# Strassen products of eight expert rounds put in another order, one round's weight sums and the round count moved forward

## The chip, the cores and the metric

The kernel runs on one core of one Trainium2 chip. The metric is device time in microseconds (us) of one execution, median of several runs. The engines are named as the profile names them: PE (TensorE, matrix products), DVE (VectorE), ACT (ScalarE), POOL (GpSimd) and SP (SyncE, which only starts transfers here). Products go to PSUM, in banks of 512 fp32 columns over 128 partitions; DVE and ACT read and write them there.

## What is computed

A linear attention over 8 batches of 576 tokens, normalised, gives 4608 tokens of width 512. Each token whose skip score is positive goes to one of eight experts of two layers (512 to 1024 to 512), and the result, times a gate, is added to the token.

```python
kv = np.einsum('bhsd,bhse->bhde', k, v)
out = np.einsum('bhsd,bhde->bhse', q, kv)
x = (out / rms * g_norm)                     # then (B,H,S,D) -> (4608, 512)
do_compute = x @ w_skip > 0
xc = x[do_compute]
e_idx = np.argmax(xc @ w_gate, axis=1)       # probs: softmax of the same logits
for e in range(E):
    mask = e_idx == e
    h = np.maximum(xc[mask] @ w1[e], 0.0)
    y[mask] = gate_w[mask, None] * (h @ w2[e])
out[do_compute] = xc + y
```

## The kernel before

The first 143 us or so are the attention, the choice of an expert for each token, and the slot tables; the change leaves them alone. After that come eight rounds, one for each expert, the fullest expert first. Round r holds up to `CAPS[r]` tokens: 352, 352, 320, 288, 288, 288, 256, 256. A loop behind the rounds (`tc.For_i`) takes tokens beyond these caps in further passes; its count `n_rounds` is worked out on the device. With these inputs it makes no pass.

Round 0 uses plain products (`layer_1`, `layer_2`). Rounds 1 to 7 use Strassen's scheme with seven products in place of eight, in both layers.

**Layer 1 of such a round (`fast_1`)** goes over f = 0 to 3, four blocks of 128 hidden columns of one half, and each f owns two PSUM banks, X and Y. The token halves `lo` and `hi` (n columns each, n = half the round's tokens, so 176, 160, 144 or 128) lie side by side in a bank. Each f has seven products of two matmuls each, which this text calls by letters:

| name | product, as the code has it | goes to | then |
|---|---|---|---|
| A | `w(0,0,f)` with `x(0,lo)` | X lo | ACT copies X lo to `p1` |
| B | `ws(1,f)` with `xs(1)` | Y lo | DVE adds `p1` to Y lo; ACT copies Y lo to `u` |
| C | `ws(0,f)` with `xs(0)` | X hi | ACT copies X hi to `p5` |
| D | `ws(2,f)` with `x(1,hi)` | X hi, on top | DVE adds `u` to X hi |
| E | `w(0,1,f)` with `x(0,hi)` | Y lo, on top | DVE writes Y lo + `p5` to Y hi |
| F | `w(1,0,f)` with `x(1,lo)` | X lo, on top | ACT: Relu of all of X to `ht` |
| G | `w(1,1,f)` with `xs(2)` | Y lo, on top | ACT: Relu of all of Y to `ht` |

D adds onto what C left, so it must wait until `p5` is copied. The layer that records the order also makes a product that writes a bank wait for the last ACT or DVE instruction on that bank, even where these touched the other half of it: C waits for the copy of `p1`, F for D's add, G for E's add.

The order of work is the order of the source (`tc.manual_schedule()`), engine by engine, each engine in order. The loop in `fast_1` runs f = 0 to 4 and holds two blocks at once: A, B, C, D of block f and E, F, G of block f - 1. So PE runs, in a middle step: A(f), B(f), E(f-1), C(f), F(f-1), D(f), G(f-1). In the last step, f = 4, `between()` puts the transposes of the next round's tokens (`expert_in`, L889) ahead of G(3).

DVE has other work in the same steps: `do(work, 1)` twice per f takes from `w2_sums` (L935, the weight sums of layer 2, eight jobs), and from f = 2 on come `h_sums` (L929, four instructions that combine finished blocks of `ht`: blocks 0 and 1 after f = 2, block 2 after f = 3, block 3 after f = 4).

**Layer 2 (`fast_2`)** has the same seven products once, each of four matmuls of 256 columns, in the order A, B, C, E, D, F, G. In it DVE takes `beside`: four jobs of `x_sums` (L935) and eight of `w1_sums` (L929, each 128x512), the sums of the next round's tokens and first-layer weights. Then come, in rounds 1 to 5, the tokens beyond 256 with plain products (`layer_2`, L919). `result` (L1107) adds gate times product to the tokens on DVE, and POOL scatters them to `out` (L1110).

What the next round needs of `w1_sums`: B reads its second part, C the first, D, E and G the last ones. `held` (L997) is the ACT copy and `add` (L991) the DVE add of all of this.

Behind round 7 nine small DVE instructions work out the count (`over` to `rnd_i`, L1217 to L1232), and `values_load` (L1235) brings it into a register of each engine; the loop's branch reads it.

Of the kernel before, what the change touches and what calls it, by code (L numbers as in the profile page):

```python
# [17 lines left out]
def kernel(  # L18
# [44 lines left out]
    nc = tc.nc  # L63
# [719 lines left out]
    with tc.tile_pool(name="wpool_b", bufs=1, reuse_waits="tile") as wpool_b, \  # L783
# [216 lines left out]
        def fast_1(r, xt, ht, n, work, between):  # L1000
# [18 lines left out]
            xy = {}  # L1019
            for f in range(HF + 1):  # L1020
                now, was = f < HF, f > 0
                if now:
                    X, Y = bank(), bank()
                    product(X[:, lo], HD, w(0, 0, f), x(0, lo), True)
                    p1 = held(X[:, lo], "p1")
                    product(Y[:, lo], HD, ws(1, f), xs(1), True)
                    add(Y[:, lo], Y[:, lo], p1)
                    u = held(Y[:, lo], "u")
                if was:
                    X_, Y_, p5_ = xy.pop(f - 1)  # L1030
                    product(Y_[:, lo], HD, w(0, 1, f - 1), x(0, hi), False)
                    add(Y_[:, hi], Y_[:, lo], p5_)
                do(work, 1)
                if now:
                    product(X[:, hi], HD, ws(0, f), xs(0), False)
                    p5 = held(X[:, hi], "p5")
                    xy[f] = X, Y, p5
                if was:
                    product(X_[:, lo], HD, w(1, 0, f - 1), x(1, lo), False)
                    nc.scalar.activation(out=ht[:, f - 1, 0:2 * n], in_=X_[:, 0:2 * n], func=ACT.Relu)  # L1040
# [6 lines left out]
                if was:  # L1047
                    product(Y_[:, lo], HD, w(1, 1, f - 1), xs(2), False)
                    nc.scalar.activation(out=ht[:, HF + f - 1, 0:2 * n], in_=Y_[:, 0:2 * n],
                                         func=ACT.Relu)  # L1050
                if f == 2:
                    do(h_sums(r, ht, slice(0, 2)))
                elif f > 2:
                    do(h_sums(r, ht, slice(f - 1, f)))
            do(work)

        def fast_2(r, ht, rest, work, put):
# [73 lines left out]
        def experts(pieces, srcs, xt, ht, yps0, tables, group):  # L1131

            for r in range(E):
# [15 lines left out]
                if r == 0:  # L1149
                    if yps0 is not None:  # L1150
                        tables = first_tables(lambda fs: layer_1(r, xt, ht, slice(P, end), fs), tables)
                        result((0, P, 0), yps0, xgs[0], tables, group)
                    else:
                        layer_1(r, xt, ht, slice(0, end), range(FC))
                    enter(more)
                else:
                    fast_1(r, xt, ht, end // 2, w2_sums(r), lambda: enter(more[0:1]))
                    enter(more[1:])
                if more:
                    n = (more[-1][0] + more[-1][1]) // 2  # L1160
                    beside = x_sums(r + 1, new["xt"], n) + w1_sums(r + 1)
# [5 lines left out]
                else:  # L1167
                    of = {piece[0:2]: piece for piece in todo}
# [3 lines left out]
                if more:  # L1172
                    xt, ht = new["xt"], new_ht()

# [25 lines left out]
        def first_tables(layer, tables):  # L1200
# [3 lines left out]
            for i, t in enumerate((0, half)):  # L1204
# [9 lines left out]

        over = slot_pool.tile([P, E, E], FP32)
        cnt = count_tokens("cnt", slot_pool)
        nc.vector.tensor_tensor(out=over[:, :, :], in0=is_at[:, :, :],  # L1217
                                in1=cnt[:, :].unsqueeze(1).to_broadcast([P, E, E]), op=ALU.mult)
        at_place = slot_pool.tile([P, E], FP32)
        nc.vector.tensor_reduce(out=at_place[:, :], in_=over[:, :, :], axis=AX.X, op=ALU.add)  # L1220
        nc.vector.tensor_tensor(out=at_place[:, :], in0=at_place[:, :], in1=caps[:, :],
                                op=ALU.is_gt)
        rnd = slot_pool.tile([P, 1], FP32)
        nc.vector.tensor_reduce(out=rnd[:, :], in_=at_place[:, :], axis=AX.X, op=ALU.max)
        cmx = slot_pool.tile([P, 1], FP32)
        nc.vector.tensor_reduce(out=cmx[:, :], in_=cnt[:, :], axis=AX.X, op=ALU.max)
        more = slot_pool.tile([P, ROUNDS], FP32)
        nc.vector.tensor_scalar(out=more[:, :], in0=full[:, :], scalar1=cmx[:, 0:1],
                                scalar2=rnd[:, 0:1], op0=ALU.is_lt, op1=ALU.mult)
        nc.vector.tensor_reduce(out=rnd[:, :], in_=more[:, :], axis=AX.X, op=ALU.add)  # L1230
        rnd_i = slot_pool.tile([P, 1], I32)
        nc.vector.tensor_single_scalar(out=rnd_i[:, :], in_=rnd[:, :], scalar=1.0, op=ALU.add)  # L1232
        order.__exit__(None, None, None)

        n_rounds = nc.values_load(rnd_i[0:1, 0:1], min_val=1, max_val=ROUNDS + 1)  # L1235
# [51 lines left out]
```

## Time and profile before

| | us |
|---|---|
| median of 3 runs | 442.76 |
| lowest and highest | 441.32, 446.06 |
| the profiled execution, its time | 440.08 |
| its span, first to last instruction | 438.3 |
| PE busy in the span | 368.8 |
| DVE busy | 250.3 |
| ACT busy | 136.8 |
| POOL busy | 120.6 |
| start of round 1's first product | 193.03 |
| start of the last add of results on DVE | 425.52 |

A row of the timeline gives start, length, engine, line, operation, the tile written and those read, the shape, and how many equal instructions it merges; in brackets stands how long the engine had idled before and what ended that. PE is the matmul, PEld the weight load ahead of it. Each fp32 matmul of the program appears as two in the trace, so a product of layer 1 is a row "x4" and one of layer 2 a row "x8"; neighbours of one form are merged. The length of a PE row is modelled and overlaps the next row, so a product's cost is read from one start to the next.

### The profile page before, as it was taken

Reading aid. Unit: us, or ns where it says so; the run is one execution under the profiler, and the core shown is the slowest. Engines: PE = TensorE matmul, PEld = TensorE weight load, DVE = VectorE, ACT = ScalarE, POOL = GpSimd, SP = SyncE. Lnnn points to the kernel's source line nnn. Section 1 sums busy time; section 2 is a strip of 40 time slices with the busy share of each in tenths; the row PEclk is TensorE's granted clock in tenths of the full one; section 3 lists DMA queues with packets and bytes.
Section 4 is the critical chain, followed back from the end, with each engine's and each line's share of the span. In section 5 each row is a group of like instructions: output and inputs, shape, how many; then the busy total and the mean of one; then the engine's idle time right before and its main releaser. Section 6 shows DMA issues by size and latency. Waiting matters only on the chain.

```text
span 438.3 us, 10443 instructions
## 1 busy us (share of the span) xinstructions
PE 368.8 (84%) x4281; PEld 315.4 (72%) x4281; DVE 250.3 (57%) x621; ACT 136.8 (31%) x365; POOL 120.6 (28%) x185
## 2 busy tenths in 40 slices
PE   0689998698754989989999999999999999997870
PEld 0578886586643949659878887888888888887760
DVE  2115577459896651175655656756656657747530
ACT  1146675446542221203302411421421412413200
POOL 3005677336549060032021303203203103201010
PEclk9869999879785799999999999999999999999995
DMA  7899999974449980635326255455455346201000
GB/s 244 304 390 389 400 399 377 289 276 99 99 133 404 298 295 13 216 99 193 113 104 221 67 194 165 141 191 160 137 192 179 115 191 206 87 1 49 0 24 24
DMA packets 32791, 81.95 MB, mean 187 GB/s; under 512 B 3326, under 2 KB 3330, under 8 KB 32736
## 3 DMA queue, kind: packets, MB, share of 16 engines
q1 hardware_dynamic: 26656, 66.59, 43.2%
q0 software_dynamic: 4576, 14.54, 10.2%
q8 instruction: 35, 0.57, 0.6%
q10 hardware_dynamic: 1504, 0.08, 0.2%
q14 instruction: 20, 0.16, 0.1%
HBM read 66.87 MB, written 14.61 MB: 186 GB/s over the span
## 4 chain that ended last, share of the span: by engine, by line
PE 68%; DVE 15%; issue 4%; DMA 4%; ACT 3%; POOL 2%; DVEq 0%; POOLq 0%; ACTq 0%
PE bank L987 38%; PE bank L919 6%; PE o_ps L402 6%; PE bank L908 5%; PE sum_ps L300 4%; PE q_ps L362 3%; DMA q<-in_q_dram 3%; DVE bank L991 2%; DVE xl L431 2%; DVE hs L929 2%; DVE s L929 2%; DMA wraw<-in_moe_w_gate_dram 2%; DVE w L929 1%; PE g_ps L329 1%; DVE t L935 1%
## 5 line engine op out<-in xcount | busy, mean ns | idle before, releaser
L1110 POOL DMA_INDIRECT out_dram<-xg,rows x16 | 17.4, 1085 | 167.4 <-DVE xg L1107 166.7
L987 PE MATMUL bank<-xt,w 128*128 128x144 f32 (+3 forms) x336 | 55.3, 291 | 0.0
L997 ACT COPY p<-bank 128x144 f32<-128x144 f32 (+4 forms) x70 | 21.0, 300 | 106.1 <-PE bank L987 104.8
L987 PEld LDWEIGHTS bank<-xt,w 128*128 128x128 f32 x336 | 47.0, 191 | 1.4 <-issue 1.4
L991 DVE TENSOR_TENSOR bank<-bank,p 128x144 f32<-128x144 f32 (+4 forms) x70 | 23.0, 338 | 33.1 <-PE bank L987 31.6
L402 PEld LDWEIGHTS o_ps<-kvn,qT 64*64 64x64 f32 (+1 forms) x384 | 28.6, 174 | 15.8 <-issue 7.4
L402 PE MATMUL o_ps<-kvn,qT 64*64 64x73 f32 (+1 forms) x384 | 34.2, 273 | 6.6 <-DVE xl L431 6.2
L464 POOL TENSOR_TENSOR xb<-xl,g_b 128x512 f32<-128x512 f32 x32 | 38.0, 1187 | 0.2 <-issue 0.2
L987 PE MATMUL bank<-xs,s 128*128 128x144 f32 (+3 forms) x224 | 37.6, 292 | 0.2 <-ACT p L997 0.2
L300 PE MATMUL sum_ps<-v,k 64*64 64x64 f32 x1152 | 25.7, 245 | 13.1 <-DMA v<-in_v_dram 10.6
L402 PE MATMUL o_ps<-kvs,qT 64*64 64x73 f32 (+1 forms) x384 | 33.3, 273 | 3.0 <-issue 3.0
L919 PE MATMUL bank<-w,ht 128*32 128x128 f32 (+2 forms) x448 | 34.7, 320 | 0.0
L414 DVE TENSOR_REDUCE rs<-sq 128x8 f32<-128x512 f32 x36 | 24.5, 679 | 17.8 <-ACT sq L406 17.3
L300 PEld LDWEIGHTS sum_ps<-v,k 64*64 64x64 f32 x1152 | 22.6, 156 | 16.1 <-issue 15.3
L987 PEld LDWEIGHTS bank<-xs,s 128*128 128x128 f32 x224 | 31.5, 191 | 1.4 <-ACT p L997 0.6
L879 POOL DMA_INDIRECT xg<-out_dram,src x15 | 15.8, 1052 | 54.2 <-PE bank L987 32.1
L431 DVE TENSOR_TENSOR xl<-o_ps,rs 128x584 f32<-128x584 f32 x36 | 27.6, 767 | 4.8 <-PE g_ps L321 0.5
L987 PE MATMUL bank<-w,ht 128*128 128x256 f32 x112 | 27.2, 386 | 3.7 <-DVE bank L991 3.7
L919 PEld LDWEIGHTS bank<-w,ht 128*32 128x32 f32 (+2 forms) x448 | 21.0, 121 | 12.9 <-issue 9.9
L987 PE MATMUL bank<-xt,s 128*128 128x144 f32 (+3 forms) x112 | 21.5, 314 | 9.5 <-ACT p L997 7.1
L402 PEld LDWEIGHTS o_ps<-kvs,qT 64*64 64x64 f32 (+1 forms) x384 | 27.8, 173 | 0.6 <-ACT rs L421 0.4
L991 DVE TENSOR_TENSOR bank<-bank,u 128x144 f32<-128x144 f32 (+4 forms) x35 | 11.9, 341 | 27.4 <-PE bank L987 27.4
(181 smaller groups left out, 725.7 us busy)
## 6 DMA issues: line engine op xcount, KB each, us to landing
w<-in_moe_w_dram SPq DMA_DIRECT2D x16, 2048.0 KB, 9.2
k<-in_k_dram SPq DMA_DIRECT2D x8, 1152.0 KB, 13.5
v<-in_v_dram SPq DMA_DIRECT2D x8, 1152.0 KB, 15.5
q<-in_q_dram SPq DMA_DIRECT2D x8, 1152.0 KB, 15.9
out_dram<-xb SPq DMA_DIRECT2D x8, 512.0 KB, 9.0
out_dram<-xb POOLq DMA_DIRECT2D x8, 512.0 KB, 7.4
out_dram<-x SPq DMA_DIRECT2D x2, 256.0 KB, 8.5
out_dram<-x POOLq DMA_DIRECT2D x2, 256.0 KB, 6.5
```

The costliest lines, as they stand in the source:

```text
L300: nc.tensor.matmul(out=sum_ps[w * 64:(w + 1) * 64, a, u, :], lhsT=kt[r, 2 * u + w, c, :], rhs=vt[r, 2 * u + w, c, :], start=(c == 0), stop ...
L402: nc.tensor.matmul(out=ps[to, r, cols], lhsT=lhsT, rhs=kv[rows, u, a * KD:(a + 1) * KD], start=True, stop=True, skip_group_check=True)
L414: nc.vector.tensor_reduce(out=rs[:, :, :], in_=sq[:, :, :, :].rearrange("p r w (a d) -> p r (w a) d", a=2), axis=AX.X, op=ALU.add)
L431: nc.vector.tensor_tensor(out=xl[:, :, :, :].rearrange("p r w (a k) -> p r (w a) k", a=2), in0=ps[:, :, 0:2 * PK].rearrange("p r (h k) -> ...
L464: nc.gpsimd.tensor_tensor(out=xb[:, :, 4 * u * D:(4 * u + 4) * D].rearrange("p r (w x) -> p r w x", w=2), in0=xl[:, :, :, G:G + 2 * D], in ...
L908: nc.tensor.matmul(out=hps[:, cols], lhsT=w_sb[r][0][:, dc, f * P:(f + 1) * P], rhs=xt[:, dc, cols], start=(dc == 0), stop=(dc == DC - 1))
L919: nc.tensor.matmul(out=yps[q * m:(q + 1) * m, 0:n], lhsT=ht[:, f, off:off + m], rhs=w_sb[r][1][:, f, q * n:(q + 1) * n], start=(f == 0), s ...
L929: yield lambda to=to, x=x, y=y, op=op: nc.vector.tensor_tensor(out=s[to], in0=x, in1=y, op=op)
L987: nc.tensor.matmul(out=out, lhsT=lhsT(i), rhs=rhs(i), start=start and i == 0, stop=i == k - 1, skip_group_check=True)
L991: nc.vector.tensor_tensor(out=to, in0=x, in1=y, op=ALU.add)
L997: nc.scalar.copy(out=t, in_=x)
L1110: ins = nc.gpsimd.indirect_dma_start(out=cut_rows(m)[:, :], out_offset=bass.IndirectOffsetOnAxis(ap=rows[:, col:col + 1], axis=0), in_=x, ...
```

## The change

Four things change; no arithmetic does.

- In `fast_1`, D of a block moves one step back: the loop now runs A, B, C of block f and D, E, F, G of block f - 1, and PE's order in a middle step is A(f), B(f), D(f-1), E(f-1), C(f), F(f-1), G(f-1). In the last step the transposes come behind F(3), ahead of G(3), with D(3) and E(3) ahead of both. The second `do(work, 1)` of a step stands behind G.
- In `fast_2`, F moves ahead of D: A, B, C, E, F, D, G.
- `w1_sums(1)` runs in round 0 directly behind the first `result`, ahead of the transposes and of layer 2; it used to be the second part of `beside`, among layer 2's pieces. Later rounds keep it in `beside`.
- The count is worked out in round 1, ahead of `fast_2`, in a function `rounds()` with the same nine instructions, and `values_load` stands in round 7 ahead of `fast_2`.

```diff
@@ fast_1
             for f in range(HF + 1):
-                now, was = f < HF, f > 0
+                now, g = f < HF, f - 1
                 if now:
                     X, Y = bank(), bank()
...
-                    u = held(Y[:, lo], "u")
-                if was:
-                    X_, Y_, p5_ = xy.pop(f - 1)
-                    product(Y_[:, lo], HD, w(0, 1, f - 1), x(0, hi), False)
-                    add(Y_[:, hi], Y_[:, lo], p5_)
+                    us[f] = held(Y[:, lo], "u")
+                if g >= 0:
+                    X_, Y_ = banks[g]
+                    product(X_[:, hi], HD, ws(2, g), x(1, hi), False)
+                    add(X_[:, hi], X_[:, hi], us.pop(g))
+                    product(Y_[:, lo], HD, w(0, 1, g), x(0, hi), False)
+                    add(Y_[:, hi], Y_[:, lo], p5s.pop(g))
                 do(work, 1)
                 if now:
                     product(X[:, hi], HD, ws(0, f), xs(0), False)
...
-                if now:
-                    product(X[:, hi], HD, ws(2, f), x(1, hi), False)
-                    add(X[:, hi], X[:, hi], u)
-                else:
-                    between()
+                    if not now:
+                        between()
+                    product(Y_[:, lo], HD, w(1, 1, g), xs(2), False)
...
                 do(work, 1)
-                if was:
-                    product(Y_[:, lo], HD, w(1, 1, f - 1), xs(2), False)
@@ fast_2
             do(work, 1)
+            product(X[:, lo], HF, h(1, 0), w(1, lo), False)
+            do(work, 2)
             product(X[:, hi], HF, hs(2), w(1, hi), False)
             add(X[:, hi], X[:, hi], u)
-            do(work, 2)
-            product(X[:, lo], HF, h(1, 0), w(1, lo), False)
             put((0, P), X)
@@ experts
+                    do(w1_sums(r + 1))
                     enter(more)
...
-                    beside = x_sums(r + 1, new["xt"], n) + w1_sums(r + 1)
+                    beside = x_sums(r + 1, new["xt"], n) + (w1_sums(r + 1) if r else [])
...
+                    if yps0 is not None and r == 1:
+                        rnd_i = rounds()
+                    if yps0 is not None and r == E - 1:
+                        n_rounds.append(nc.values_load(rnd_i[0:1, 0:1], min_val=1,
+                                                       max_val=ROUNDS + 1))
                     of = {piece[0:2]: piece for piece in todo}
                     fast_2(r, ht, todo[2:], beside,
```

PE, round 7, the step f = 1 of layer 1; the number of a bank tells X and Y of the two blocks apart. Before, X and Y of block 0 are 4260 and 4261, those of block 1 are 4280 and 4281:

```order
L987 MATMUL bank_4260<-xt_4053,s1_4197 128x128 x2
L987 MATMUL bank_4280<-xt_4053,w1_4046 128x128 x2
L987 MATMUL bank_4281<-xs_4196,s1_4197 128x128 x2
L987 MATMUL bank_4261<-xt_4053,w1_4046 128x128 x2
L987 MATMUL bank_4280<-xs_4196,s1_4197 128x128 x2
L987 MATMUL bank_4260<-xt_4053,w1_4046 128x128 x2
L987 MATMUL bank_4280<-xt_4053,s1_4197 128x128 x2
L987 MATMUL bank_4261<-xs_4196,w1_4046 128x128 x2
```

Now block 0 has 4276 and 4277, block 1 has 4293 and 4294:

```order
L987 MATMUL bank_4293<-xt_4069,w1_4062 128x128 x2
L987 MATMUL bank_4294<-xs_4212,s1_4213 128x128 x2
L987 MATMUL bank_4276<-xt_4069,s1_4213 128x128 x2
L987 MATMUL bank_4277<-xt_4069,w1_4062 128x128 x2
L987 MATMUL bank_4293<-xs_4212,s1_4213 128x128 x2
L987 MATMUL bank_4276<-xt_4069,w1_4062 128x128 x2
L987 MATMUL bank_4277<-xs_4212,w1_4062 128x128 x2
```

Before, D(0) (the first row) stood ahead of A(1), right behind C(0), and D(1) (the seventh row) two places behind C(1). Now D(0) is the third row, behind A(1) and B(1), and F(0) and G(0) close the step.

DVE, round 4, from the sums of blocks 0 and 1 (hs, 128x256) to those of block 2 (hs, 128x128); "bank<-bank,p" is an add of B or E, "bank<-bank,u" one of D. Before:

```order
L929 TENSOR_TENSOR hs<-ht,hs 128x256
L991 TENSOR_TENSOR bank<-bank,p_3893 128x144
L991 TENSOR_TENSOR bank<-bank,p_3873 128x144
L935 TENSOR_TENSOR t_3805<-w_3546,t_3805 128x512
L991 TENSOR_TENSOR bank<-bank,u 128x144
L935 TENSOR_TENSOR t_3805<-w_3546,t_3805 128x512
L929 TENSOR_TENSOR hs<-ht 128x128
L929 TENSOR_TENSOR hs<-hs,ht 128x128
L929 TENSOR_TENSOR ht<-ht 128x128
L929 TENSOR_TENSOR hs<-ht,hs 128x128
L991 TENSOR_TENSOR bank<-bank,p_3906 128x144
```

Now:

```order
L929 TENSOR_TENSOR hs<-ht,hs 128x256
L991 TENSOR_TENSOR bank<-bank,p_3906 128x144
L991 TENSOR_TENSOR bank<-bank,u 128x144
L991 TENSOR_TENSOR bank<-bank,p_3889 128x144
L935 TENSOR_TENSOR t_3821<-w_3562,t_3821 128x512 x2
L929 TENSOR_TENSOR hs<-ht 128x128
L929 TENSOR_TENSOR hs<-hs,ht 128x128
L929 TENSOR_TENSOR ht<-ht 128x128
L929 TENSOR_TENSOR hs<-ht,hs 128x128
L991 TENSOR_TENSOR bank<-bank,u 128x144
L991 TENSOR_TENSOR bank<-bank,p_3922 128x144
```

The add of D(3), ahead of the sums of block 2 before, now stands behind them, directly ahead of E(3)'s.

DVE, from the first results of round 0 to the first add of round 1 (L991); s is the tile of `w1_sums`. Before:

```order
L1107 SCALAR_TENSOR_TENSOR xg_211<-bank,gate,xg_211 128x512 x2
L935 TENSOR_TENSOR xs<-xt 128x2x176
L935 TENSOR_TENSOR xs<-xt,xs 128x2x176
L935 TENSOR_TENSOR xt<-xt 128x2x176
L935 TENSOR_TENSOR xs<-xt,xs 128x2x176
L1107 SCALAR_TENSOR_TENSOR xg_211<-bank,agate,xg_211 128x256
L929 TENSOR_TENSOR s_2694<-w_2530 128x512 x2
L929 TENSOR_TENSOR s_2694<-s_2694,w_2530 128x512 x2
L1107 SCALAR_TENSOR_TENSOR xg_211<-bank,agate,xg_211 128x128
L929 TENSOR_TENSOR w_2530<-w_2530 128x512 x2
L929 TENSOR_TENSOR s_2694<-w_2530,s_2694 128x512 x2
L991 TENSOR_TENSOR bank<-bank,p_2794 128x176
```

Now:

```order
L1106 SCALAR_TENSOR_TENSOR xg_211<-bank,gate,xg_211 128x512
L929 TENSOR_TENSOR s_2674<-w_2530 128x512 x2
L929 TENSOR_TENSOR s_2674<-s_2674,w_2530 128x512 x2
L929 TENSOR_TENSOR w_2530<-w_2530 128x512 x2
L929 TENSOR_TENSOR s_2674<-w_2530,s_2674 128x512 x2
L1106 SCALAR_TENSOR_TENSOR xg_211<-bank,gate,xg_211 128x512
L935 TENSOR_TENSOR xs<-xt 128x2x176
L935 TENSOR_TENSOR xs<-xt,xs 128x2x176
L935 TENSOR_TENSOR xt<-xt 128x2x176
L935 TENSOR_TENSOR xs<-xt,xs 128x2x176
L1106 SCALAR_TENSOR_TENSOR xg_211<-bank,agate,xg_211 128x256
L1106 SCALAR_TENSOR_TENSOR xg_211<-bank,agate,xg_211 128x128
```

The eight jobs of `w1_sums` that stood between the last pieces of round 0 and the first add of round 1 now stand behind the first result.

More of the change, by code (lines that the diff above doesn't have):

```diff
@@ L1035, in fast_1 @@
                     product(X[:, hi], HD, ws(0, f), xs(0), False)
[L1036 to L1045 removed]
+                    p5s[f] = held(X[:, hi], "p5")
+                if g >= 0:
+                    product(X_[:, lo], HD, w(1, 0, g), x(1, lo), False)
+                    nc.scalar.activation(out=ht[:, g, 0:2 * n], in_=X_[:, 0:2 * n], func=ACT.Relu)
+                    if not now:
+                        between()
+                    product(Y_[:, lo], HD, w(1, 1, g), xs(2), False)
+                    nc.scalar.activation(out=ht[:, HF + g, 0:2 * n], in_=Y_[:, 0:2 * n],
+                                         func=ACT.Relu)
                 do(work, 1)
[L1047 to L1050 removed]
                 if f == 2:
@@ L1212 @@
         experts(plan, (src, asrc), xt0, ht0, yps0, (rows, arows), "first")
[L1215 to L1232, printed above, removed]
         order.__exit__(None, None, None)
-        n_rounds = nc.values_load(rnd_i[0:1, 0:1], min_val=1, max_val=ROUNDS + 1)
+        n_rounds = n_rounds[0]
         colid = slot_pool.tile([P, NCOL], I32)
```

25 lines of the change are left out of this document (24 added, 1 removed).

## Prediction

> **What bounds the kernel now.** I read the page first, for the share of each engine and for the chain that ended last.
>
> ```profile
> PE 368.8 (84%) x4281; PEld 315.4 (72%) x4281; DVE 250.3 (57%) x621; ACT 136.8 (31%) x365; POOL 120.6 (28%) x185
> ...
> PE 68%; DVE 15%; issue 4%; DMA 4%; ACT 3%; POOL 2%; DVEq 0%; POOLq 0%; ACTq 0%
> PE bank L987 38%; PE bank L919 6%; PE o_ps L402 6%; PE bank L908 5%; PE sum_ps L300 4%; PE q_ps L362 3%; DMA q<-in_q_dram 3%; DVE bank L991 2%; DVE xl L431 2%; DVE hs L929 2%; DVE s L929 2%; DMA wraw<-in_moe_w_gate_dram 2%; DVE w L929 1%; PE g_ps L329 1%; DVE t L935 1%
> ```
>
> PE carries the chain, and the Strassen products (L987) alone are 38% of it. The DVE pieces in the chain (L991, hs, s, w, t) are the places where PE stood still between those products. The view of waits on PE says what for:
>
> ```profile
> PE bank L987 <- ACT p L997: 7.4, 13, 2.4
> PE bank L987 <- DVE bank L991: 6.6, 14, 0.9
> PE bank L987 <- DVE t L935: 2.3, 1, 2.3
> ```
>
> That is 16.3 us in 28 waits. The true loss is larger: a matmul row is modelled, and the wait and the restart are better seen from start to start. So I read the timeline of PE in one round, round 4, with n = 144.
>
> ```profile
> 333.65 1.34 PE L987 MATMUL bank<-xs,s 128*128 128x144 f32 x8
> 335.52 0.76 PE L987 MATMUL bank<-xt,s 128*128 128x144 f32 x4 [0.52 <-ACT p L997]
> ...
> 341.21 0.65 PE L987 MATMUL bank<-xs,s 128*128 128x144 f32 x4
> 341.70 0.65 PE L987 MATMUL bank<-xt,w 128*128 128x144 f32 x4
> 342.29 0.76 PE L987 MATMUL bank<-xt,s 128*128 128x144 f32 x4
> 342.89 0.65 PE L987 MATMUL bank<-xs,w 128*128 128x144 f32 x4
> ...
> 345.34 0.65 PE L987 MATMUL bank<-xt,w 128*128 128x144 f32 x4
> 346.35 0.76 PE L987 MATMUL bank<-xt,s 128*128 128x144 f32 x4 [0.36 <-ACT p L997]
> 346.94 0.65 PE L987 MATMUL bank<-xs,w 128*128 128x144 f32 x4
> ...
> 348.41 0.60 PE L889 MATMUL bank<-ident,xg 128*128 128x128 f32 x4
> 349.38 0.76 PE L987 MATMUL bank<-xs,w 128*128 128x144 f32 x4 [0.37 <-DVE bank L991]
> 349.97 0.60 PE L889 MATMUL bank<-ident,xg 128*128 128x128 f32 x4
> 350.41 1.89 PE L987 MATMUL bank<-w,ht 128*128 128x256 f32 x8
> ...
> 355.59 1.89 PE L987 MATMUL bank<-t,ht 128*128 128x256 f32 x8
> 357.32 1.89 PE L987 MATMUL bank<-w,hs 128*128 128x256 f32 x8
> 359.73 2.00 PE L987 MATMUL bank<-w,ht 128*128 128x256 f32 x8 [0.52 <-DVE bank L991]
> 361.56 1.89 PE L987 MATMUL bank<-t,ht 128*128 128x256 f32 x8
> ```
>
> An undisturbed product takes one step of 0.49 us (341.21 to 341.70). Every "xt,s" row is a D, behind F in the old order (behind C in the first step). What each place loses, in order:
>
> - D(0) was due two steps after 333.65, at 334.63, and came at 335.52: 0.9 late.
> - D(2) came 0.59 after F(1), and the product behind it 0.60 after D(2): 0.10 of waiting and 0.10 of restart, 0.20. D(1) is the same case.
> - D(3) came 1.01 after F(2): 0.52, with the restart 0.62.
> - G(3) came 0.97 after four transposes, which take 0.44 (349.97 to 350.41): 0.53, with the restart 0.63.
> - In layer 2 a step is 1.73 (355.59 to 357.32). F came 2.41 behind D, and G 1.83 behind F: 0.68 and 0.10, so 0.78.
>
> **The change, part by part. Layer 2.** F waits for D's add because both use bank X. With F ahead of D nothing of that is left: the next product on D's bank is in no hurry, G writes Y, and E's add on Y has D and F ahead of it, two steps. The add of D and the result of X then lie beside G's 1.73 us. Seven rounds at 0.78: **5.5 us gone**. What is late next is the result of Y behind G, as now.
>
> **The start of a round.** D(0) waits for a chain on DVE and ACT (last weight sums, B(0)'s add, copy u, copy p5). Now A(1) and B(1) stand ahead of it, two steps of work. Round 4 had 0.9 to hide and gets 0.98 of cover. Round 7 has more than that:
>
> ```profile
> 395.17 1.29 PE L987 MATMUL bank<-xs,s 128*128 128x128 f32 x8
> 398.81 0.71 PE L987 MATMUL bank<-xt,s 128*128 128x128 f32 x4 [2.35 <-ACT p L997]
> 399.36 0.61 PE L987 MATMUL bank<-xt,w 128*128 128x128 f32 x4
> ...
> 193.73 1.64 PE L987 MATMUL bank<-xs,s 128*128 128x176 f32 x8
> 197.68 0.86 PE L987 MATMUL bank<-xt,s 128*128 128x176 f32 x4 [2.31 <-DVE t L935]
> 198.38 0.76 PE L987 MATMUL bank<-xt,w 128*128 128x176 f32 x4
> ```
>
> In round 7 the step is 0.45 (0.55 from 398.81 to 399.36, less 0.10), D(0) is 2.7 late, and two steps cover 0.9 of it. I take 0.9 for each of rounds 2 to 7: **5.4 us**. The lower end is 0, if the products that now stand in the gap are themselves held up.
>
> Round 1 (the last three rows) has a step of 0.60, so D(0) was due at 194.93 and came at 197.68: 2.75, with the restart 2.85. There the weight sums themselves leave the boundary.
>
> ```profile
> 143.40 1.66 SPq L271 DMA_DIRECT2D w<-in_moe_w_dram  x1
> ...
> 187.65 0.75 DVE L1107 SCALAR_TENSOR_TENSOR xg<-bank,gate,xg 128x512 f32<-128x512 f32 x1 [7.29 <-PE bank L919]
> ...
> 191.67 1.28 DVE L929 TENSOR_TENSOR s<-w 128x512 f32<-128x512 f32 x2
> ```
>
> Eight sums at 0.64 are 5.1 us, and their new place is the 7.29 us in which DVE idled ahead of 187.65. Their weights were asked for at 143.40, 37 us before that idle time begins. So they are hidden, and **2.85 us go**. If the weights were late, DVE would stand in front of the next result and the term would fall towards 0; the distance of 37 us speaks against it.
>
> **Inside layer 1.** D(1), D(2), D(3) have four products between them and their copy now, so 0.20, 0.20 and 0.62 go, and so does G(3)'s 0.63: 1.65 a round. Two new waits come. F now needs D's add, and G needs E's add, each three steps earlier.
>
> ```profile
> 343.16 0.32 DVE L991 TENSOR_TENSOR bank<-bank,u 128x144 f32<-128x144 f32 x1 [0.84 <-PE bank L987]
> ...
> 345.49 0.52 DVE L991 TENSOR_TENSOR bank<-bank,p 128x144 f32<-128x144 f32 x2
> ```
>
> From D(2)'s start at 342.29 to the end of its add at 343.48 are 1.19, of which 0.10 is the restart: 1.09 against three steps of 1.47. With DVE free this costs nothing; DVE is not free behind the block sums. (a) In step 3 the adds of B(3) and D(2) come behind the sums of blocks 0 and 1, which end at 345.49, 2.60 after G(1). Two adds take 0.52, the way to PE 0.06: F(2) can start 3.18 after G(1), and is due six steps, 2.94, after it: 0.24, with the restart 0.34. (b) In step 4 the add of D(3) comes behind the sums of block 2. Today the first product behind those is G(3), 2.44 after G(2) (346.94 to 349.38). Now it is F(3), due three steps, 1.47, after G(2): 0.97, with the restart 1.07, and the transposes that softened it stand behind F(3). So 1.41 a round comes back, 0.24 is left, and over seven rounds **1.7 us go**. The bounds are 11.6 (none of the new waits) and a loss of 3.8 (both twice as long, against 1.65 gone).
>
> Row 349.38 shows the place where a rule bears on this: the product waits for an add that itself waits behind sums it does not need. The Trainium skill, TensorE: Matmul & The Clock Gate, section on the array's architectural detail, says that VectorE's queue is strictly first in, first out. By that rule the 1.07 in step 4 stands, and with it the sum below; if DVE could take D(3)'s add first, seven times 1.07 more would go and the time would be 420.5. The trace agrees with the rule.
>
> **The count.** On each engine a register load is added ahead of layer 2 of round 7, and nine small DVE instructions move into layer 2 of round 1, where DVE waits for the first product anyway; I cost those at nothing.
>
> ```profile
> L1235 PEldq TENSOR_LOAD <-rnd_i x1: 736/736/736, 428.1 to 428.1; - x1
> ...
> 426.54 0.98 POOL L1110 DMA_INDIRECT out_dram<-xg,rows  x1 [0.74 <-DVE cnt L595]
> ...
> DMA to landing us min/median/max: 2.6/3.3/7.7
> ...
> L1238 POOLq EVENT_SEMAPHORE  x16: 17/43/96, 429.0 to 432.3; - x16
> ```
>
> PE's queue stands still for the load, 0.74, with nothing beside it: **0.7 us added** (0 if queued matmuls cover it, 1.5 if the restart doubles it). At the end I expect no gain: POOL reaches its waits for transfers at 429.0, and the last scatter, issued at 426.54, lands at 429.1 at the earliest by the shortest landing, 2.6. Without the count POOL would only wait there longer.
>
> **The sum.** 5.5 + 5.4 + 2.85 + 1.7 - 0.7 = 14.7 us. The profiled execution took 440.08, which gives 425.4. It lies 2.7 below the median of the three runs shown, 442.76, and the change should be seen there: **428.0 us**.
>
> **Rivals.**
>
> - *The starts give back what they gain.* DVE now has two weight sums between B(0)'s add and B(1)'s; if the products behind D(0) then wait for them, 5.4 us stay: 433.4. Against it: D(0)'s add is due about 1.1 after D(0), and two sums of 0.68 fit ahead of it. 0.14.
> - *The three-step window is too short* (slower). F and G wait in each of 28 blocks, 56 times. The spare time is 1.47 - 1.15 = 0.32, for n = 128 about 0.27. It decides where the way from a product to the next one over DVE is longer than three steps: each 0.1 beyond costs 0.2 with the restart, 11 us in all, and 0.34 a time makes the kernel slower than 447. The rows give 1.15 with DVE free, so this needs DVE behind in every block, and it is behind only after the block sums. 0.04.
> - *The clock.* The view of stretches has the granted clock ahead of the last two columns: half in parts of the attention, whole in the rounds:
>
> ```profile
> 83.00:94.00 11.00, 9.71 (x174) 8.42 (x174) 3.60 (x10) 3.72 (x11) 3.66 (x7) 0.53 1.03 381
> ...
> 333.00:350.00 17.00, 15.75 (x124) 14.58 (x118) 12.31 (x32) 6.51 (x20) 3.65 (x4) 1.00 0.55 173
> ```
>
> Ten us at half clock cost about 5 us of PE time; three such stretches in the rounds would eat the gain, 443. 0.03. The Trainium skill, same page, Part 1, says that activity releases the clock and idle windows lower it; by that rule a PE that waits less keeps its clock and this rival is out. No round here tests it.
>
> - *The end is shorter after all*: the nine instructions and the load leave POOL's path, 1.3 us from 427.5 to 428.8: 426.7. The landing speaks against it. 0.08.
> - *The new waits inside layer 1 are milder*, half of 1.41 in each of seven rounds: 423.1. 0.06.
>
> **How the numbers follow.** The main case has 0.65, with a range of its own of 425.5 to 430.5. The range for all, 423.5 to 433.5, reaches to the starts that give nothing on one side and most of the way to the milder waits on the other; the two bounds of the load lie inside. Something over 1% (4.4 us) can be told from no change here. Faster by more than that is every case but the window and the clock, less a little for a sum of small misses: 0.92; within 1%: 0.04; slower: 0.04.
>
> **What would show it.** F 1.73 behind E and D 1.73 behind F in layer 2, with no wait; D(0) of round 1 without a wait, of rounds 2 to 6 too, and of round 7 with some 1.7 left; D(1) to D(3) with none. New waits of F(3), about 1 us a round, for DVE, and smaller ones of F(2) from round 3 on. The last scatter to the end of the span as long as before, 11.8 us. The prediction is wrong if F and G wait in steps 1 and 2, if D(0) still waits in rounds 2 to 6, or if a round runs below the full clock.

## The result, and the profile after

| | before | changed |
|---|---|---|
| median, us | 442.34 of 4 runs | 429.49 of 4 runs |
| lowest, highest | 441.32, 446.06 | 428.29, 432.58 |
| profiled execution, its span | 440.08, 438.3 | 429.86, 428.1 |
| round 1's first product to the end of the span | 245.3 | 230.8 |

The ratio is 0.9705, 95% interval 0.9629 to 0.9782: faster, and 1.5 us above the 428.0 forecast, inside the main case's own range.

The last row of the table is worked out from the first product A(0) of round 1. These are the rows of the timeline of PE, the first of the kernel before, the others of the changed one:

```profile
193.03 0.86 PE L987 MATMUL bank<-xt,w 128*128 128x176 f32 x4
```

```profile
197.31 0.86 PE L987 MATMUL bank<-xt,w 128*128 128x176 f32 x4
...
199.86 0.76 PE L987 MATMUL bank<-xs,s 128*128 128x176 f32 x4
200.46 0.76 PE L987 MATMUL bank<-xt,s 128*128 128x176 f32 x4
```

A(0) started 4.3 us later in the changed kernel's profile. The sums that were moved into round 0 did not do that: from the first product of round 0's second layer to A(0) are 37.37 us in both (155.66 to 193.03 before, 159.94 to 197.31 now), so the delay comes from ahead of it. In the twelve other profiles read below and above A(0) started anywhere from 192.3 to 199.9. The profiled run of e8, below, was a slow one (435.79 us), but what it lost lies ahead of its A(0) at 199.92, and its layer 1 took the 117.1 of the changed kernel. That scatter lies in every median; the time behind A(0) does not have it, and there the change won 245.3 - 230.8 = **14.5 us**, against 14.7 in the forecast's sum. The row at 200.46 is D(0), 0.60 behind B(1) (199.86), as every product there: no wait is left in it.

The view of waits on PE had 28 waits and 16.3 us on these products before, now:

```profile
PE bank L987 <- DVE bank L991: 6.0, 9, 0.8
PE bank L987 <- ACT p L997: 1.5, 1, 1.5
```

The timeline of PE in round 5 shows which. (The rows that the prediction showed for n = 144 and called round 4 are round 5's as well; rounds 3 to 5 have the same sizes.)

```profile
330.56 0.65 PE L987 MATMUL bank<-xs,s 128*128 128x144 f32 x4
331.05 0.65 PE L987 MATMUL bank<-xt,s 128*128 128x144 f32 x4
331.54 0.65 PE L987 MATMUL bank<-xt,w 128*128 128x144 f32 x4
...
338.89 0.65 PE L987 MATMUL bank<-xs,s 128*128 128x144 f32 x4
339.62 0.76 PE L987 MATMUL bank<-xt,w 128*128 128x144 f32 x4
...
341.20 0.65 PE L987 MATMUL bank<-xt,w 128*128 128x144 f32 x4
342.66 0.76 PE L987 MATMUL bank<-xt,w 128*128 128x144 f32 x4 [0.81 <-DVE bank L991]
...
349.80 1.89 PE L987 MATMUL bank<-t,ht 128*128 128x256 f32 x8
351.53 1.89 PE L987 MATMUL bank<-w,ht 128*128 128x256 f32 x8
353.25 1.89 PE L987 MATMUL bank<-w,hs 128*128 128x256 f32 x8
354.98 1.89 PE L987 MATMUL bank<-t,ht 128*128 128x256 f32 x8
```

D(0) at 331.05 comes one step of 0.49 behind B(1) and E(0) one step behind it: the start waits for nothing. F(2) at 339.62 is 0.24 late, F(3) at 342.66 comes 1.46 behind E(3), 0.97 late; with the restart of 0.10 that is 0.34 and 1.07, the two new waits of the forecast to the digit. In layer 2 E, F, D, G follow each other at 1.73.

From starts like these, the length of each layer in each round, in us (layer 2 with the plain products behind it, in round 7 up to the start of its last matmul):

| | r1 | r2 | r3 | r4 | r5 | r6 | r7 | sum |
|---|---|---|---|---|---|---|---|---|
| layer 1 before | 21.76 | 18.49 | 17.57 | 17.45 | 17.35 | 16.58 | 17.71 | 126.90 |
| layer 1 changed | 18.92 | 17.61 | 16.43 | 16.43 | 16.32 | 15.32 | 16.07 | 117.12 |
| layer 2 before | 18.46 | 16.58 | 14.86 | 14.86 | 14.86 | 12.88 | 12.66 | 105.17 |
| layer 2 changed | 17.67 | 15.79 | 14.07 | 14.07 | 14.07 | 12.09 | 11.87 | 99.62 |

Layer 1 won 9.8, layer 2 5.5, together 15.3. Since 14.5 came out, 0.8 were lost behind the last product. The view of transfers, cut to the time from the last scatter's issue to its landing, shows it; before, and below it changed:

```profile
q0 software_dynamic: 145, 0.37, 36.4%
issues: line engine op xcount, KB each, median us to landing
out_dram<-xg,rows POOLq DMA_INDIRECT x1, 2.6
```

```profile
q0 software_dynamic: 160, 0.43, 33.8%
q8 instruction: 1, 0.02, 1.6%
q14 instruction: 1, 0.01, 0.5%
issues: line engine op xcount, KB each, median us to landing
out_dram<-xg,rows POOLq DMA_INDIRECT x1, 3.4
```

The columns behind a queue are packets, MB and share of time. With the count in the registers early, the branches behind the rounds run early and fetch their code (the two rows "instruction") while the scatter is under way; it lands after 3.4 and not 2.6. From the moment POOL sees the landing to the end of the span both have 9.1.

### The profile page after: what moved, and what is told of

Its sections match the earlier page's. It is cut to its first block, busy times and chain, and to the rows that moved or that the text cites. A ratio compares the mean times of both kernels' runs of the same rounds, so it can differ in the third digit from the quotient of the medians.

```text
span 428.1 us, 10435 instructions
## 1 busy us (share of the span) xinstructions
PE 360.0 (84%) x4281; PEld 313.1 (73%) x4281; DVE 249.8 (58%) x621; ACT 137.4 (32%) x365; POOL 120.8 (28%) x185
## 5 line engine op out<-in xcount | busy, mean ns | idle before, releaser
L987 PE MATMUL bank<-xt,w 128*128 128x144 f32 (+3 forms) x336 | 57.7, 294 | 6.2 <-DVE bank L991 6.0
L991 DVE TENSOR_TENSOR bank<-bank,p 128x144 f32<-128x144 f32 (+4 forms) x70 | 23.6, 337 | 36.5 <-PE bank L987 35.7
L879 POOL DMA_INDIRECT xg<-out_dram,src x15 | 16.7, 1113 | 53.5 <-PE bank L987 31.7
L919 PEld LDWEIGHTS bank<-w,ht 128*32 128x32 f32 (+2 forms) x448 | 21.0, 121 | 12.9 <-issue 9.9
L448 POOL TENSOR_TENSOR lp<-xl 128x36 f32<-128x36 f32 x36 | 9.2, 255 | 70.6 <-DVE xl L431 70.3
L365 ACT COPY qT<-q_ps 128x512 f32<-128x512 f32 x32 | 18.8, 587 | 28.4 <-PE q_ps L362 28.2
L406 ACT ACTIVATE sq<-o_ps 128x512 f32<-128x512 f32 x36 | 21.5, 597 | 19.5 <-PE o_ps L402 19.3
```

What stands on the lines that cost most here:

```text
L365: nc.scalar.copy(out=qT[:, :, :, :].rearrange("p w a t -> p (w a t)"), in_=ps[:, :, :, :, :].rearrange("p w a h t -> p (w a h t)"))
L406: nc.scalar.activation(out=sq[:, :, :, :], in_=heads(ps, G, G + 2 * D), func=ACT.Square)
L919: nc.tensor.matmul(out=yps[q * m:(q + 1) * m, 0:n], lhsT=ht[:, f, off:off + m], rhs=w_sb[r][1][:, f, q * n:(q + 1) * n], start=(f == 0), s ...
L987: nc.tensor.matmul(out=out, lhsT=lhsT(i), rhs=rhs(i), start=start and i == 0, stop=i == k - 1, skip_group_check=True)
L991: nc.vector.tensor_tensor(out=to, in0=x, in1=y, op=ALU.add)
```

## The experiments

Eleven runs followed, e11 the changed kernel once more. The table has what was measured, in us; "part" is round 1's first product to the end of the span, "end" the last scatter's issue to the end of the span, both of the profiled run.

| kernel | median | ratio to before, 95% | part | layer 1 | layer 2 | end |
|---|---|---|---|---|---|---|
| changed | 429.49 | 0.963 to 0.978 | 230.8 | 117.1 | 99.6 | 12.6 |
| e1_count_late | 424.83 | 0.954 to 0.970 | 230.0 | 117.1 | 99.6 | 11.8 |
| e2_l2_old | 431.19 | 0.969 to 0.983 | 236.2 | 117.1 | 105.2 | 12.5 |
| e3_l1_old | 435.82 | 0.976 to 0.993 | 240.1 | 126.4 | 99.7 | 12.6 |
| e4_sums_back | 427.20 | 0.960 to 0.973 | 232.3 | 118.7 | 99.6 | 12.5 |
| e5_sums_behind | 422.56 | 0.942 to 0.955 | 227.8 | 110.8 | 103.0 | 12.5 |
| e6_sums_early | 427.16 | 0.953 to 0.967 | 232.8 | 115.5 | 103.3 | 12.5 |
| e7_both | 420.59 | 0.939 to 0.954 | 225.6 | 108.4 | 103.3 | 12.4 |
| e8_load_late | 430.86 | 0.958 to 0.973 | 234.0 | 117.1 | 103.0 | 12.4 |
| e9_best | 416.63 | 0.937 to 0.947 | 220.6 | 107.7 | 99.6 | 11.8 |
| e10_delay | 425.20 (1 run) | - | 230.7 | 117.1 | 99.6 | 12.5 |
| e11_changed_again | 425.75 | 0.958 to 0.969 | 230.3 | 117.1 | 99.6 | 12.1 |

They ran in three groups, e1 to e4, e5 to e8 and e9 to e11, each on one chip with its own runs of the kernel before. e5 to e8 all have 1.1 us more in layer 2 of each of rounds 3 to 5; e8, whose rounds are those of the changed kernel, has it too, so e5 to e7 are set against e8 and its 234.0.

**The parts one by one. e1_count_late** undoes the early count:

```diff
-                    if yps0 is not None and r == 1:
-                        rnd_i = rounds()
-                    if yps0 is not None and r == E - 1:
-                        n_rounds.append(nc.values_load(rnd_i[0:1, 0:1], min_val=1,
-                                                       max_val=ROUNDS + 1))
...
+        rnd_i = rounds()
         order.__exit__(None, None, None)
...
-        n_rounds = n_rounds[0]
+        n_rounds = nc.values_load(rnd_i[0:1, 0:1], min_val=1, max_val=ROUNDS + 1)
```

> The changed kernel with the count alone put back: its nine DVE instructions behind the last result, its register loads behind everything. Three theories of the early count. (a) It brings nothing at the end and costs 0.7 us on PE, as forecast: then the time from round 1's first product to the end of the span becomes 230.1, 0.7 less than the 230.8 of the changed kernel. (b) The load lies under the queued matmuls and costs nothing, but the branches now fetch their code while the last scatter is under way and hold its landing up: then layer 2's first product still starts one step, 0.45, behind the last product of layer 1 in round 7, as it does with the load in between; the last scatter lands 2.6 behind its issue as in the kernel before, not 3.4, and from its issue to the end of the span are 11.8, not 12.6; 230.0. (c) The landing varies by itself and the early count is worth nothing either way: 230.8, with a landing anywhere between 2.6 and 3.6, and kernels that keep the early count show landings of 2.6 too.

Theory (b) in each number: the part is 230.0, the end 11.8, the landing 2.6, and no instruction fetch lies between issue and landing. Layer 1 is as long without the load as with it, so the load cost nothing.

**e2_l2_old** has the old `fast_2`, D ahead of F.

> The changed kernel with layer 2 alone in the old order, F behind D. The theory: F waits for D's add in each of seven rounds, 0.78 a round with the restarts, and nothing else moves: 5.5 us slower than the changed kernel, some 435. The rival is that the starts of the rounds take part of it back, since the sums beside layer 2 get 0.78 more time: then D(0) of round 7 waits less, 1.0 in place of 1.7, and the loss is 4.8. The last scatter keeps the early count: by the collision it lands 3.4 behind its issue again, by chance alone anywhere from 2.6.

Layer 2 is the kernel before's to the hundredth, 105.17, and layer 1 the changed kernel's, round 7 (16.07) among it: 5.4 us in the part, and nothing handed on to the starts. Its last scatter landed after 3.3, again with a code fetch beside it.

**e3_l1_old** has the old `fast_1`.

> The changed kernel with layer 1 alone in the old order, D ahead of the copies of the next step. The theory: the starts of rounds 2 to 7 lose their 5.0 us again, and the inside of layer 1 its 1.9; round 1, whose weight sums have left the boundary, loses little at its start, 0.2 to 0.9 in place of 2.85: 7 to 8 us slower than the changed kernel, some 437. The rival, that the weight sums alone did the whole work of round 1, has the start of round 1 as good as in the changed kernel, and the loss at 6.9; that the order of layer 1 did it has the start 2.8 slower and the loss at 9.7.

9.4 us, more than the theory's 7 to 8. Round 1 lost 0.71 (19.63 to 18.92): neither 0 nor 2.8, so the moved sums and the new order shared that start. The view of the timeline, D(0) of round 1:

```profile
196.20 1.42 PE L987 MATMUL bank<-xs,s 128*128 128x176 f32 x8
198.02 0.86 PE L987 MATMUL bank<-xt,s 128*128 128x176 f32 x4 [0.39 <-ACT p L997]
```

Two steps of 0.60 behind the first row would be 197.39; it is 0.63 late, and 0.10 go to the restart. Rounds 2 to 6 lost 5.4. Round 7 lost 3.2, and half of that has another cause. First two rows of its timeline, then the view of stretches, with the granted clock ahead of the last two columns:

```profile
394.44 0.71 PE L987 MATMUL bank<-xt,s 128*128 128x128 f32 x4 [2.36 <-ACT p L997]
...
396.27 1.06 PE L987 MATMUL bank<-xt,w 128*128 128x128 f32 x4
```

```profile
394.40:398.80 4.40, 4.36 (x24) 4.36 (x25) 2.19 (x6) 0.80 (x3) 0.00 (x0) 0.62 0.00 0
```

Behind D(0)'s wait of 2.36 the clock fell to 0.62 on average, and four products took 0.85 apiece in place of 0.45: 1.6 us. Without that the loss is 7.8, inside the theory's band. Last, the load. Here G(3) had waited, and the load began with it; the load, then the products:

```profile
L1172 PEldq TENSOR_LOAD <-rnd_i x1: 488/488/488, 408.9 to 408.9; - x1
```

```profile
408.91 0.71 PE L987 MATMUL bank<-xs,w 128*128 128x128 f32 x4 [0.85 <-DVE bank L991]
409.62 1.97 PE L987 MATMUL bank<-w,ht 128*128 128x256 f32 x8
```

Layer 2 starts 0.71 behind G(3), where a step and a restart are 0.55: the same load of 0.49 that costs nothing in the changed kernel costs 0.16 here.

**e4_sums_back** puts `w1_sums(1)` back into `beside`.

> The changed kernel with round 1's weight sums back at the boundary. The theory: the two products that now stand ahead of D(0) cover two steps of 0.60 of the 2.75 that it was late, so D(0) of round 1 waits 1.55 and 0.1 for the restart: 1.65 us slower than the changed kernel. The rival: the order of layer 1 alone covers all of it and moving the sums was worth nothing: 0. The other rival: the products that stand in the gap are held up too: 2.85 slower.

Round 1's layer 1 took 20.52 for 18.92, 1.6, and nothing else moved: the theory. So of the 2.84 won in round 1 the order alone is worth 1.24 (21.76 to 20.52), the sums alone 2.13 (21.76 to 19.63), and they overlap by half a us: each hides part of the same wait.

**What delays the last scatter. e8_load_late** computes the count early and loads it behind the rounds.

> The changed kernel with the count computed early but loaded into the registers at the end, as in the kernel before. It tells which half of the early count delays the last scatter. If it is the branches, which run as soon as the registers are loaded: 11.8 from the last scatter's issue to the end of the span and a landing after 2.6, and 230.0 from round 1's first product. If it is the moved DVE instructions: 12.6, with a landing after 3.4, and 230.8.

12.4, as with the early load. The run did not decide: with the count known since round 1 the loads waited for nothing, so they and the branches still ran ahead of the scatter. **e10_delay** makes them wait:

```diff
...
+        wide = slot_pool.tile([P, 512], FP32, name="wide")
+        nc.vector.memset(wide[:, :], 0.0)
+        for _ in range(3):
+            nc.vector.tensor_tensor(out=wide[:, :], in0=wide[:, :], in1=wide[:, :], op=ALU.add)
+        rnd_i = slot_pool.tile([P, 1], I32)
+        nc.vector.tensor_single_scalar(out=rnd_i[:, :], in_=n_rounds[0][:, :], scalar=1.0, op=ALU.add)
...
```

> The changed kernel with eight of the count's nine DVE instructions early, the ninth and the register loads at the end behind some 2 us of idle work on DVE (a fill and three additions on 128x512, which no result uses). If the code that the branches fetch is what delays the last scatter: the fetch comes after the last packet, the packets end 2.3 behind the issue and not 2.8 to 3.0; from the issue to the end of the span 11.8, or more by as much as the idle work outlasts the landing. If the early DVE instructions or the loads in themselves are the cause: 2.8 to 3.0 again.

The view of transfers from issue to landing, the loads' rows under it:

```profile
q0 software_dynamic: 160, 0.43, 42.4%
issues: line engine op xcount, KB each, median us to landing
out_dram<-xg,rows POOLq DMA_INDIRECT x1, 2.6
```

```profile
L1247 PEldq TENSOR_LOAD <-rnd_i x1: 488/488/488, 413.5 to 413.5; - x1
```

Eight of the nine DVE instructions are early, the loads come 2.5 behind the issue (410.99), no fetch lies beside the packets, and they land after 2.6. So the fetched code delays the scatter, not the DVE instructions. Nor do the loads: in the changed kernel the last of them began at 403.5, 12 us ahead of the scatter. The end is 12.5 all the same, since the idle work outlasts the landing. Of the profiles, each with the branches early has an end of 12.1 to 12.6 and a fetch beside the packets; each with the count late (before, e1, e9) has 11.8 and none.

**What the new waits are. e5_sums_behind** puts the block sums behind the adds:

```diff
                     add(Y_[:, hi], Y_[:, lo], p5s.pop(g))
-                do(work, 1)
+                    if g > 0:
+                        do(h_sums(r, ht, slice(g - 1, g)))
+                do(work, 2)
...
-                if f == 2:
-                    do(h_sums(r, ht, slice(0, 2)))
-                elif f > 2:
-                    do(h_sums(r, ht, slice(f - 1, f)))
+            do(h_sums(r, ht, slice(HF - 1, HF)))
```

> The changed kernel with the block sums of h behind the adds: the sums of block f - 1 come in step f + 1 (block 0 in step 2, 1 in step 3, 2 in step 4) behind D's and E's adds and not ahead of them, and the weight sums of w2 are all issued by step 2. The theory: F(2) and F(3) wait only because D(2)'s and D(3)'s adds stand behind those sums in DVE's queue, so both waits go: 7.4 us for F(3) and 2.2 for F(2) over the seven rounds, 9.6 in all; 221.2 from round 1's first product to the end of the span. Rival one: the adds wait for PE and ACT and not for the sums; then nothing changes, 230.8. Rival two: block 2's sums now push block 3's back, and the second product of layer 2, which needs them, waits; at one block's sums, 1.05, a round, 7.4 come back and 228.6 are left.

No wait for the adds is left in the view, and layer 2 waits for no sums: both rivals fall. But 6.2 us were won (against e8), not 9.6. The timeline of PE in round 5, then that of DVE:

```profile
335.68 0.65 PE L987 MATMUL bank<-xt,s 128*128 128x144 f32 x4
336.17 1.40 PE L987 MATMUL bank<-xt,w 128*128 128x144 f32 x8
337.41 0.60 PE L889 MATMUL bank<-ident,xg 128*128 128x128 f32 x4
```

```profile
335.36 0.28 DVE L929 TENSOR_TENSOR hs<-ht,hs 128x128 f32<-128x128 f32 x1
336.44 0.32 DVE L991 TENSOR_TENSOR bank<-bank,u 128x144 f32<-128x144 f32 x1 [0.79 <-PE bank L987]
336.93 0.32 DVE L991 TENSOR_TENSOR bank<-bank,p 128x144 f32<-128x144 f32 x1 [0.17 <-PE bank L987]
337.16 0.28 DVE L929 TENSOR_TENSOR hs<-ht 128x128 f32<-128x128 f32 x1
```

DVE now idles ahead of D(3)'s add at 336.44. E(3) and F(3) are merged in the row at 336.17, and the transposes come 1.24 behind its start where two steps are 0.98: 0.26 of F(3) stays. In the last step no A, B, C stand between; F(3) is only two steps behind D(3), 0.98 against the 1.09 to 1.15 of the way over DVE. Seven times 0.25 are 1.8 of the missing 3.4. Another 1.2 came back in rounds 6 and 7 (0.68 and 0.78 won in place of 1.33, the two waits of 1.61 less the 0.28 that stays): there three sums of w2 now stand ahead of B(1)'s and D(0)'s adds, and F(0) comes 0.3 and 0.4 late with its restart. The transposes of round 6 come 0.3 late too, and the load in round 7 costs 0.15: it began at 395.3, hardly ahead of G(3) at 395.36, and layer 2 starts 0.60 behind G(3) where a step is 0.45. Some 0.3 are a late F(0) in rounds 3 to 5.

**e6_sums_early** issues all sums for the next round inside layer 2, four each behind A, B and E.

> The changed kernel with the sums for the next round (four of x, eight of w1) all issued inside layer 2, four behind each of A, B and E, and none behind the last result. The theory: D(0) of round 7 waits 1.63 and 0.1 for the restart because four sums are left over behind round 6's results, so it goes: 1.7 us faster, 229.1. A second part: the 0.1 of C at the start of rounds 2 to 6 goes with it, 0.5 more. The rival: the larger blocks of sums now stand ahead of E's and D's adds in layer 2 and G or the results wait, 0.1 to 0.6 a round: between nothing and 3 us slower.

Round 7's layer 1 fell from 16.07 to 14.34, the 1.73 of the theory; C's 0.1 stayed. Round 1's layer 2 rose by 0.29, E waiting for the larger block once, and layer 1 of round 4 by 0.15: 1.2 net in the part.

**e7_both** has the two.

> Both of these together, on the changed kernel. If they are independent: 9.6 and 1.7 to 2.2 us, some 219.3 from round 1's first product to the end of the span, PE with no wait of over 0.2 us left in the rounds. The rival is that DVE becomes the bound: PE no longer gives it the time that it lost in waits, 1.4 a round, and waits show up at the starts of the rounds; then 2 to 7 us less are won.

8.4 us against e8: all that the two won alone (7.4) and 1.0 more, but 3 less than the 11.3 to 11.8 expected. The loss is not that of the rival: the view of waits on PE lists none for DVE in the rounds, and D(0) of round 7 comes one step behind B(1). Of the missing 3 us, 1.8 are the 0.25 of F(3) in seven rounds, which e5 had left already. The two are independent, and DVE did not become the bound.

**e9_best** takes e7 and adds the late count, one sum of w2 fewer in step 0, and the first transposes ahead of F(3) (the lines of e5, e6 and the count are left out here):

```diff
-                do(work, 1)
...
+                do(work, 2 if f else 1)
...
                 if g >= 0:
+                    if not now:
+                        between()
                     product(X_[:, lo], HD, w(1, 0, g), x(1, lo), False)
                     nc.scalar.activation(out=ht[:, g, 0:2 * n], in_=X_[:, 0:2 * n], func=ACT.Relu)
-                    if not now:
-                        between()
```

> A version meant to beat both: the sums behind the adds and early in layer 2 as in the kernel before this one, the count at the end, the first four transposes of the next round ahead of F(3) and not behind it, so that D(3)'s add has two products and 0.44 us of transposes to end in, and one sum of w2 fewer in step 0. On the other hand the time from round 1's first product to the end of the span was 225.6 for the two moves alone on a chip on which three pauses of 1.05 in the small products of rounds 3 to 5 are part of it. The theory: 0.25 a round of F(3) goes in six rounds, 1.5; up to 0.4 of F(0) in each of rounds 6 and 7; 0.7 at the end: 222.6 with the pauses, 219.4 without. The rival is that G(3) or the sums of the last block are now late and layer 2's second product waits: 0.2 to 0.5 a round back, some 225.

The median is 416.63, ratio 0.9419 (0.9369 to 0.9470), and the changed kernel on the same chip 425.75: it beats the kernel before and the changed one. The part is 220.6 where 219.4 was expected. The row of busy shares on its page, then all that the view of waits on PE lists in the rounds:

```profile
PE 359.1 (86%) x4281; PEld 313.5 (75%) x4281; DVE 254.0 (61%) x649; ACT 138.1 (33%) x365; POOL 119.4 (29%) x185
```

```profile
PE bank L889 <- DMA xg<-out_dram,src: 0.8, 2, 0.5
```

What is late next is the gather of the next round's tokens, for which the transposes now wait; round 6 took 15.15 where e7 had 14.49, and in rounds 6 and 7 F(2) comes 0.2 late again.

**e11_changed_again** is the changed kernel once more.

> The changed kernel itself, on the chip of the two kernels before. From round 1's first product to the end of the span 230.8 if the chip has no pauses in the small products of rounds 3 to 5, 234.0 if it has them; the packets of the last scatter end 2.8 to 3.0 behind its issue; layer 1 of the seven rounds takes 117.1 in all either way. If the rounds of the changed kernel vary from run to run by more than 0.3, the differences read so far are less sure than they look.

Layer 1 was 117.13 and layer 2 99.62, against 117.12 and 99.62, and no round differs by more than 0.03. Differences of 0.1 between rounds can be trusted. The end was 12.1 and the landing 3.0, so the fetch costs between 0.3 and 0.8 from run to run; its packets ended 2.5 behind the issue, earlier than expected.

## Why the prediction was right

| term of the sum | forecast | measured |
|---|---|---|
| layer 2, seven rounds | 5.5 | 5.5 |
| start of round 1 | 2.85 | 2.8 |
| starts of rounds 2 to 7 | 5.4 | 5.0 |
| inside layer 1 | 1.7 | 1.9 |
| register load on PE | -0.7 | 0 |
| the end | 0 | -0.8 (-0.3 in e11) |
| sum | 14.7 | 14.5 |

The measured terms are rounded; the 14.5 is 245.3 - 230.8.

**Layer 2** held in each number, and e2 shows it stands alone. **Round 1**: the forecast had the sums do it all; e3 and e4 show the sums worth 2.1 alone and the order 1.2. The number held because the order hides the 0.7 that the sums alone would have left; the forecast did not count on that, so here it was lucky. **Rounds 2 to 7**: each start won 0.7 to 0.95. The step "I take 0.9 for each" was too large by C's own restart of 0.10, which the forecast took to go and which stays. Round 7 kept a wait, now 1.63 and the restart, as said:

```profile
388.11 0.61 PE L987 MATMUL bank<-xs,s 128*128 128x128 f32 x4
390.19 0.71 PE L987 MATMUL bank<-xt,s 128*128 128x128 f32 x4 [1.47 <-ACT p L997]
```

**Inside layer 1** the two new waits came where and as long as worked out; in rounds 1 and 2 they were smaller (no F(2) wait in round 1), in 6 and 7 larger. That they hang on the order of DVE's queue was argued from one row; e5 shows it: with the sums behind the adds both go, down to the 0.25 that the two steps leave. That F(3) stands only two steps behind D(3) the forecast did not see; behind the longer wait for the sums it made no difference. The Trainium skill, TensorE: Matmul & The Clock Gate, section on the array's architectural detail, has VectorE's queue as strictly first in, first out; the runs agree.

**The load** was the mis-sized term. "PE's queue stands still for the load, 0.74, with nothing beside it" failed: the rows of the changed kernel, the load first,

```profile
L1171 PEldq TENSOR_LOAD <-rnd_i x1: 485/485/485, 401.4 to 401.4; - x1
```

```profile
401.73 0.61 PE L987 MATMUL bank<-xs,w 128*128 128x128 f32 x4
402.17 1.89 PE L987 MATMUL bank<-w,ht 128*128 128x256 f32 x8
```

have it at 401.4, ahead of G(3)'s own start, with F(3) still running and G(3) queued; layer 2 starts one step of 0.45 behind G(3). The bound 0 was the value here, but not in general: where the load began with G(3) or hardly ahead of it (e3, e5) it cost 0.15. It also took 0.49, not 0.74.

**The end** failed on its other side: "without the count POOL would only wait there longer" was right, but the landing itself became 0.8 longer, which no case held. The two misses cancel within 0.1, and that is luck. The Trainium skill, Runtime: NRT & Kernel Launch, section on instruction fetch mechanics, says that a taken branch out of the window forces a fetch by DMA before execution can go on. The trace agrees that the fetch comes; that it slows another transfer is shown by e1 and e10 alone.

Of the rivals, the starts gave nothing back, the window of three steps held in every middle step (it fails only in the last step, where F(3) has two), and the waits were not milder. The granted clock was 1.00 from 197 to 415 in the changed kernel; e3 shows what a fall costs. That the median gained 12.9 and not 14.5 is put down to the scatter ahead of A(0), which no run tests by itself: the same kernel beside other runs of before, in e11, has a median 16.8 lower (442.56 to 425.75).

## What to carry to other kernels

Count how many products stand between a write to a bank and the next product that needs it, and put as many there as the way over the other engine takes: two steps of 0.5 us were too few here, three enough. Then look at what stands ahead of that small add in its own engine's queue; sums that nobody waits for yet belong behind it, and that move won 6.2 us here, beside the change's 14.5. Work taken from the end of a kernel wins nothing if the last transfer ends it anyway, and may cost if it starts other traffic beside that transfer.

## What the runs showed of the hardware that was not expected

- A code fetch (0.02 and 0.01 MB in the changed kernel) beside the last scatter lengthens that scatter from 2.6 us to between 3.0 (e11) and 3.5 (e3).
- A register load of 0.49 us on PE, placed between G(3) and layer 2 of round 7, cost nothing where it began 0.3 ahead of G(3) (changed kernel, 401.4 and 401.73), 0.15 where it began just ahead of it (e5, 395.3 and 395.36), and 0.16 where it began with it (e3, 408.9).
- In e3 a wait of 2.36 us was followed by some 3.4 us at half clock (0.62 on average over 4.40); in the kernel before the same wait of 2.35 in the same round was not. The Trainium skill, TensorE: Matmul & The Clock Gate, Part 1, names an idle window of about 3.4 us as what brings the half clock, and says that the window runs freely; the second fits that one fell and the other did not, but the wait was shorter than the length it names.
- On the chip of e5 to e8 PE lost some 1.1 us in the last sixteen of the 64 small products of rounds 3, 4 and 5 each, in all four kernels; on the other chips never. e8, timeline of PE:

```profile
330.12 1.72 PE L919 MATMUL bank<-w,ht 128*32 128x128 f32 x50
332.00 0.44 PE L919 MATMUL bank<-w,ht 128*32 128x128 f32 x6 [0.17 <-issue]
332.73 0.47 PE L919 MATMUL bank<-w,ht 128*32 128x128 f32 x8 [0.29 <-issue]
```

The profile puts the idle time down to issue, not to another engine or a transfer; its cause stays open and was not tried.
